# Block-sparse attention with a feed-forward layer: an ordering edge from the newest exponential on ScalarE to the score and AV groups on TensorE

## The chip, the cores and the metric

The kernel runs on one core of a Trainium2 chip, as one program. The metric is the device time of one execution in microseconds. Engines are named as in the profile: PE is TensorE (PEld its weight loads), DVE is VectorE, ACT is ScalarE, POOL is GpSimd, SP issues most DMAs. Each engine works through its own list of instructions in order; engines wait for one another by semaphores.

## The reference

```
B, H, S, D = 4, 8, 768, 64          # q, k, v; blocks of 32, 24 blocks
mask: |blk_i - blk_j| <= 1, or either block first or last, or one of 3 sampled blocks per row of blocks
scores = where(mask, q @ k.T / sqrt(D), -1e9)
attn = softmax(scores)              # exp(scores - max) / (sum + 1e-9)
x = (attn @ v) as (B*S, 512)
h = x @ w_in                        # 512 -> 2048
out = maximum(0.01 * h, h) @ w_out  # 2048 -> 512, float32
```

## The kernel before, in words

**Tiling.** Two blocks of queries (64 rows) form a tile T, 12 per batch; T = 0 holds the first and the last block, which see all 768 keys, and the 11 others see 12 gathered blocks, 384 keys. Four T of a batch make an item (256 rows), so there are 12 items. A *unit* is one T with two heads, on 128 partitions; an item has 16 units. Two units that follow one another are a *pair*: 96 pairs in all. float32 precision is kept by splitting operands into a high and a low half of 16 bits.

**A pair's way through the engines.** `scores` (line 637, matmul on line 659): per unit four matmuls of 384 keys into one PSUM bank; there are two banks (`ps_s`, two buffers), so the scores of a pair can only be written after DVE has read those of the pair before. The second unit's matmuls are emitted first. `unit_ttr` (line 666, DVE) adds the mask, scales, takes the row's extreme and leaves the result in `p`. `unit_exp` (line 677, ACT) takes the exponential of `p` with its sum. `pair_norm` (line 685, DVE), `unit_high` (line 695, ACT) and `unit_split` (line 699, DVE) make normalised probabilities `pp` in two halves; a transposing DMA (line 704, SP) turns them into `pt`, three buffers. `pair_av` (line 730, PE) multiplies by the gathered values `vg` with 24 matmuls per pair (12 per unit) into the one PSUM bank `av`, which collects the two pairs of a T. `tile_evac` (lines 737 to 748) turns a finished T into a part of the item's `x`.

**Side work.** POOL copies sampled key blocks into `kg` (line 602, two buffers), and gathers the value blocks into `vg` by indirect DMAs (line 628, two buffers; each frees when the last AV of its T is done). q, k and v of what comes next are scaled, split and transposed (`prep_q`, `prep_k`, `prep_v`); the transposes and copies of q go by DMA (lines 546 to 549). In the first part of the run the weights are decoded, scaled and split (lines 325 to 390).

**Feed-forward (FFN).** Per item eight chunks: `ffn_h` (line 765, 24 matmuls into a bank `h`), activation on ACT, DVE and POOL (lines 771 to 779) into `g`, and `ffn_o` (line 792, 12 matmuls). An item's chunks are emitted once its attention is complete and the weights they need are ready.

**What sets the order.** The outer loop (line 1041) goes over the units, one step each; a string of letters fixes what a step emits: normalise, DVE read, split, high half, exponential (`x`), scores of the next pair (`S`, in a pair's second step), activations of FFN, `ffn_o`, evacuation, AV (`a`), side work, `ffn_h`. AV of a pair comes six steps after the pair's second unit (`av_lag` and the stages before it), so the exponential that was emitted last is then that of the second unit three pairs further on. A planner then makes the lists of the engines when the program is built: it goes through its own estimate of time and issues, on each engine, the ready instruction of the best priority. Priorities follow the order of emission. The function `together` (line 164) emits a group of matmuls: the first with the priority of its place, the others with a much better one and each tied to the first by an edge that is not a semaphore, so that the planner keeps the group nearly whole. An edge of the class `NoSync` bounds only the order in which the planner issues; nothing waits for it on the chip.

Of the kernel before, what the change touches and what calls it, by code (L numbers as in the profile page):

```python
# [65 lines left out]
def tile_block_sparse_attention_ffn(  # L66
# [19 lines left out]
    nc = tc.nc  # L86
# [30 lines left out]
    def bank(name, tag="h"):  # L117
        return ps_1.tile([P, 512], F32, tag=tag, name=name, bufs={"h": 3, "av": 1}[tag])
# [42 lines left out]
        tc.cur_priority = now + 8  # L161
        return r

    def together(emits):

        now = tc.cur_priority
        begin = len(nc.cur_bb.bb.instructions)
        for n, emit in enumerate(emits):
            if n == 1:
                tc.cur_priority = now - 100000  # L170
            emit()
        new = nc.cur_bb.bb.instructions[begin:]
        for i in new[1:]:
            tc.add_manual_dep(i, new[0].name, mybir.DependencyInfo(
                mybir.DependencyClass.NoSync, mybir.DependencyReason.DATA), reason="together")
        tc.cur_priority = now + len(new)
# [378 lines left out]
    def score_scale(b, j, i, hp):  # L555

        first = j == 0 and i == 0
        hs = slice(hp, hp + 1) if first else slice(0, NP)
        nsc = sm.tile([P, NP], F32, tag="nsc", name=f"nsc_{b}_{j}_{i}_{hp}", bufs=6)
        nc.vector.tensor_scalar(  # L560
            out=nsc[:, hs], in0=kready[b, "inv"][:, hs], scalar1=qstack[b, j, i][2][:, :1], scalar2=None, op0=ALU.mult)
        for h in range(NP)[hs]:
            nscale[b, j, i, h] = nsc[:, h:h + 1]
# [73 lines left out]
    def scores(us):  # L637

        emits = []
        for u in us:  # L640
            i, c0 = u.k // 2, u.k % 2 * Q2
            require_qk(u.b, u.j, i, u.hp)
            if u.T:
                require_kg(u.b, u.T)
            key = (u.b, u.j, i, u.hp)
            if key not in nscale:
                score_scale(*key)
            u.nsc = nscale[key]
            u.sp = [ps_s.tile([P, 512], F32, tag="s", name=f"s_{u.nm}_{part}")[:, :KEYS] for part in range(u.parts)]
        for u in us[::-1]:  # L650
            i, c0 = u.k // 2, u.k % 2 * Q2
            qs, qxs, _ = qstack[u.b, u.j, i]
            for part, sp in enumerate(u.sp):
                for n, st in enumerate((qs, qxs)):
                    for hh in range(2):
                        h = 2 * u.hp + hh
                        keys = kgs[u.b, u.T][0][:, h, :] if u.T else kts[u.b][:, h, part * KEYS:(part + 1) * KEYS]
                        emits.append(lambda o=sp[hh * D:(hh + 1) * D, :], a=st[:, h, c0:c0 + Q2], k=keys, n=n:
                                     nc.tensor.matmul(o, a, k, start=(n == 0), stop=(n == 1)))  # L659
        together(emits)  # L660

    def unit_ttr(u):
        u.p = [pa.tile([P, KEYS], F32, tag="p", name=f"p_{u.nm}_{i}", bufs=CFG["p"]) for i in range(u.parts)]
# [8 lines left out]
    def unit_exp(u):  # L672

        if u.first:
            u.pair.sum = sm.tile([P, 2, 2], F32, tag="sum", name=f"sum_{u.nm}", bufs=4)
        for i in range(u.parts):
            nc.scalar.activation(  # L677
                u.p[i], u.p[i], AF.Exp, scale=-1.0, bias=u.mx[:, :1], accum_out=u.pair.sum[:, u.pi, i:i + 1])

    def pair_norm(pr):  # L680
        tot = pr.sum[:, :, 0]
        if pr.units[0].parts == 2:
            nc.vector.tensor_tensor(out=tot, in0=tot, in1=pr.sum[:, :, 1], op=ALU.add)
        pr.r = sm.tile([P, 2], F32, tag="r", name=f"r_{pr.nm}", bufs=4)
        nc.vector.tensor_scalar(out=tot, in0=tot, scalar1=1e-9, scalar2=1.0 / PSCALE, op0=ALU.add, op1=ALU.mult)  # L685
        nc.vector.reciprocal(out=pr.r, in_=tot)
# [27 lines left out]
    def pair_av(pr):  # L714

        if pr.hp == 0:
            avs[pr.item.n, pr.T] = bank(f"av_{pr.nm}", "av").rearrange("p (n l t) -> p n l t", n=NP, l=2)
        pr.av = avs[pr.item.n, pr.T]
        for u in pr.units:
            require_v(u.b, u.hp, u.T)  # L720
        emits = []
        for u in pr.units[::-1]:
            n = NCH * u.parts
            for c in range(n):
                for l in range(2):
                    for hh in range(2):
                        vt = vgs[u.b, u.T][:, c, 2 * u.hp + hh, :] if u.T else v16s[u.b, u.hp][:, c, hh, :]
                        emits.append(lambda o=pr.av[hh * D:(hh + 1) * D, u.hp], a=vt[:, l * D:(l + 1) * D],
                                     m=u.pt[c // NCH][:, :, c % NCH, hh * D:(hh + 1) * D], c=c, l=l, n=n:
                                     nc.tensor.matmul(o, a, m, start=(c == 0 and l == 0), stop=(c == n - 1 and l == 1)))  # L730
        together(emits)

    def tile_evac(pr):

# [20 lines left out]
    def ffn_h(c):  # L755
        it = c.item
        c.ph = bank(f"h_{it.nm}_{c.f}").rearrange("p (f t) -> p f t", f=2)
        emits = []
        for i in range(2):
            f = c.f + i  # L760
            b, o = f // PER, (f % PER) * P
            for d in range(NP):
                for m, (wl, xl) in enumerate(((1, 0), (1, 1), (0, 0))):
                    emits.append(lambda i=i, d=d, m=m, w=W16[:, 2 * b, d, wl, o:o + P], x=it.x[:, xl, d, :]:
                                 nc.tensor.matmul(  # L765
                                     c.ph[:, i], w, x, start=(d == 0 and m == 0), stop=(d == NP - 1 and m == 2)))
        together(emits)
# [57 lines left out]
    for b in range(B):  # L825
        for j in range(NI):
# [3 lines left out]
            for k_ in range(TPI):  # L830
                for hp in range(0, NP, 2):
                    pr = Unit()
                    pr.item, pr.k, pr.T, pr.hp, pr.nm, pr.units = it, k_, j * TPI + k_, hp, f"{it.nm}_{k_}_{hp}", []
                    for pi in range(2):
                        u = Unit()
# [18 lines left out]
    def require_qk(b, j, i, hp):  # L854
        until(("k", b, hp), lambda: (b, hp) in kready)
        until(("q", b, j, i), lambda: (b, j, i) in qstack)

    def require_kg(b, T):
        for hp in range(NP):
            until(("k", b, hp), lambda: (b, hp) in kready)  # L860
        until(("kg", b, T), lambda: (b, T) in kgs)

    def require_v(b, hp, T):
        until(("v", b), lambda: (b, hp) in v16s if T == 0 else (b, "ready") in scr)
        while T and (b, T) not in vgs:
            start_gather_v()
# [159 lines left out]
    def av_step(now=False):  # L1026
        if pend_av and (now or pend_av[0][0] <= step):
            pr = pend_av.popleft()[1]
            tlive[0] -= pr.units[0].parts
            while evs and pr.hp == 0:  # L1030
                ev_step()
            pair_av(pr)
            if pr.hp == NP - 2:
                vfree[0] += pr.T > 0
                evs.append(tile_evac(pr))
# [5 lines left out]
    for u in units:  # L1041
# [33 lines left out]
        if step == 0:  # L1075
            scores([u])
        c = aq[0] if aq else None
        for w in CFG["ord"]:
# [7 lines left out]
            elif w == "S" and step + 1 < len(units):  # L1086
                ahead = units[step + 1:step + 3]
                if not CFG["spair"]:
                    scores(ahead[:1])
                elif u.pi == 1:  # L1090
                    if any(x.parts > 1 for x in ahead):
                        for x in ahead[:1]:
                            scores([x])
                    else:
                        scores(ahead)
                elif u.parts > 1:
                    scores(ahead[:1])
            elif w == "t":
# [6 lines left out]
                unit_ttr(u)  # L1105
            elif w == "x":
                unit_exp(u)
                if u.pi == 1:
                    pend_norm.append(u.pair)
# [95 lines left out]
```

## Time and profile before

| | |
|---|---|
| three runs | 893.37 us median, 889.02 to 898.08 |
| profiled execution | 889.45 us |
| its span, first to last instruction | 887.7 us |
| mean granted PE clock | 0.948 |
| DMA | 139.25 MB, mean 157 GB/s |

Times in the profile's views count from the start of the span. A line of the timeline gives start, duration, engine, line, operation, out<-in, how many were merged (x8), and in brackets how long the engine stood idle before it and what ended that. L659 is line 659 of the kernel before. A row of waits gives who waited for whom, total us, times, longest. `s` are the scores, `mx` the extreme that the DVE read leaves, `av` the AV bank, `qs_q` and `qxs_q` the transposed queries.

### The profile page before, as it was taken

How to read it: one execution, taken by the hardware profiler on the slowest of the kernel's cores; microseconds unless marked ns; L12 is line 12 of the kernel's file. 1: busy time of each engine (PE TensorE's matmuls, PEld its weight loads, DVE VectorE, ACT ScalarE, POOL GpSimd, SP SyncE). 2: the span in 40 equal slices, each digit the busy share in tenths (PEclk: the TensorE clock that was granted, in tenths of full speed). 3: DMA queues.
4: the chain of work that ended last, by engine and by line, in shares of the span. 5: the costliest groups of instructions: out<-in, count | busy, mean ns of one | idle time of the engine just before them, and what ended most of it. 6: DMA issues, size and time to landing. Idle time of an engine off the chain costs nothing. (4 is left out here: it accounts for less than half of the span.)

```text
span 887.7 us, 19902 instructions
## 1 busy us (share of the span) xinstructions
PE 739.8 (83%) x7020; PEld 488.9 (55%) x7020; DVE 624.9 (70%) x1623; ACT 485.8 (55%) x1063; POOL 432.7 (49%) x558
## 2 busy tenths in 40 slices
PE   0234655877999998888999999999899999999997
PEld 0213433645666665555656565656556666656674
DVE  2799898997977886773857867789657677754121
ACT  3666768665655764562645846556536454543211
POOL 0046767565236465664343475476325565633221
PEclk9999555989999999999999999999999999999999
DMA  6998999967679989893558979768836596654000
GB/s 138 272 298 192 280 208 234 207 146 170 141 165 182 197 156 194 137 212 89 145 97 157 217 145 195 169 136 184 194 59 135 106 183 154 126 100 103 20 7 25
DMA packets 328450, 139.25 MB, mean 157 GB/s; under 512 B 295453, under 2 KB 307742, under 8 KB 328350
## 3 DMA queue, kind: packets, MB, share of 16 engines
q1 hardware_dynamic: 322718, 120.67, 66.8%
q0 software_dynamic: 5632, 17.31, 7.6%
q8 instruction: 55, 0.90, 0.4%
q14 instruction: 45, 0.37, 0.1%
HBM read 65.58 MB, written 12.58 MB: 88 GB/s over the span
## 5 line engine op out<-in xcount | busy, mean ns | idle before, releaser
L792 PE MATMUL o<-W,g 128*128 128x512 f16 x1152 | 276.3, 384 | 7.9 <-DVE g L778 6.0
L765 PE MATMUL h<-x,W 128*128 128x256 f16 x2304 | 275.3, 276 | 2.4 <-DVE wi_tot L140 1.1
L765 PEld LDWEIGHTS <-W 128*128 128x128 f16 x2304 | 224.9, 100 | 51.1 <-issue 12.8
L779 POOL TENSOR_TENSOR g<-ht,g 128x512 f16<-128x512 f32 x96 | 114.8, 1196 | 216.8 <-DVE g L778 169.1
L602 POOL COPY kg<-kt 128x256 f16 x264 | 131.4, 521 | 97.0 <-PE s L659 47.7
L792 PEld LDWEIGHTS <-g 128*128 128x128 f16 x1152 | 107.7, 99 | 128.9 <-issue 14.5
L677 ACT ACTIVATE p<-p,mx 128x384 f32<-128x384 f32 x208 | 125.9, 606 | 93.0 <-DVE mx L666 70.8
L699 DVE SCALAR_TENSOR_TENSOR pp<-p,r,pp 128x384 f16<-128x384 f32 x208 | 147.9, 737 | 40.4 <-ACT pp L695 39.1
L695 ACT ACTIVATE pp<-p,r 128x384 f16<-128x384 f32 x208 | 115.6, 605 | 43.8 <-issue 12.9
L628 POOL DMA_INDIRECT vg<-scr,rows x88 | 95.0, 1080 | 61.0 <-PE av L730 40.9
L774 DVE SCALAR_TENSOR_TENSOR ht<-ht 128x512 f32<-128x512 f32 x96 | 71.1, 741 | 75.3 <-ACT ht L771 74.9
L666 DVE CUSTOM_DVE_ANT_0 p<-s,em,nsc 128x384 f32<-128x384 f32 x176 | 101.9, 611 | 25.5 <-PE s L659 25.2
L730 PE MATMUL av<-pt,vg 128*64 128x128 f16 x2112 | 84.8, 230 | 20.6 <-DMA pt<-pp 15.0
L730 PEld LDWEIGHTS <-vg 128*64 128x64 f16 x2112 | 73.5, 117 | 47.3 <-issue 41.3
L771 ACT ACTIVATE ht<-h,gd 128x512 f32<-128x512 f32 x80 | 54.1, 676 | 78.8 <-PE h L765 43.4
L659 PE MATMUL s<-kg,qs_q 128*64 128x384 f16 x352 | 65.6, 368 | 25.0 <-DVE mx L666 20.2
L659 PEld LDWEIGHTS <-qs_q 128*64 128x64 f16 x416 | 28.4, 116 | 85.1 <-issue 46.1
L659 PE MATMUL s<-kg,qxs_q 128*64 128x384 f16 x352 | 64.3, 360 | 6.3 <-DMA qxs_q<-qs_q 6.3
L778 DVE CAST g<-ht 128x512 f16<-128x512 f32 x96 | 43.9, 457 | 12.4 <-PE o L792 10.3
L748 POOL TENSOR_TENSOR x<-xf,x 128x256 f16<-128x256 f32 x48 | 37.1, 773 | 27.8 <-ACT x L746 27.3
L685 DVE TENSOR_SCALAR sum<-sum 128x2 f32<-128x2 f32 x96 | 30.9, 322 | 22.0 <-ACT p L677 21.3
L534 ACT ACTIVATE qa_q<-rq 128x512 f16<-128x512 f32 x25 | 15.7, 626 | 51.8 <-DMA rq<-in_q_dram 40.3
(129 smaller groups left out, 753.6 us busy)
## 6 DMA issues: line engine op xcount, KB each, us to landing
vg<-scr SPq DMA_DIRECT2D x44, 256.0 KB, 3.9
v<-in_v_dram SPq DMA_DIRECT2D x32, 192.0 KB, 4.5
qxs_q<-qs_q SPq DMA_DIRECT2D x48, 128.0 KB, 3.1
scr<-v SPq DMA_DIRECT2D x16, 384.0 KB, 4.2
W<-in_moe_w_in_dram SPq DMA_DIRECT2D x5, 1024.0 KB, 5.9
rq<-in_q_dram SPq DMA_DIRECT2D x20, 256.0 KB, 5.3
out_dram<-ob SPq DMA_DIRECT2D x20, 256.0 KB, 3.4
rk<-in_k_dram SPq DMA_DIRECT2D x24, 192.0 KB, 4.8
```

The source lines that it names most:

```text
L602: nc.gpsimd.tensor_copy(out=kg[:, :, slot * BLOCK:(slot + 1) * BLOCK], in_=kt[:, :, bass.ds(off, BLOCK)])
L628: nc.gpsimd.indirect_dma_start(out=vg[:n_, c, :], out_offset=None, in_=scr[b][:, :], in_offset=bass.IndirectOffsetOnAxis(ap=rows[:n_, c - ...
L659: nc.tensor.matmul(o, a, k, start=(n == 0), stop=(n == 1)))
L666: nc.vector.tensor_tensor_reduce(out=u.p[i], in0=u.sp[i], in1=kgs[u.b, u.T][1] if u.T else zero.to_broadcast([P, KEYS]), scale=u.nsc, scal ...
L677: nc.scalar.activation(u.p[i], u.p[i], AF.Exp, scale=-1.0, bias=u.mx[:, :1], accum_out=u.pair.sum[:, u.pi, i:i + 1])
L695: nc.scalar.activation(pp[:, 0, :], p, AF.Copy, scale=u.r)
L699: nc.vector.scalar_tensor_tensor(out=pp[:, 1, :], in0=p, scalar=u.r, in1=pp[:, 0, :], op0=ALU.mult, op1=ALU.subtract)
L730: nc.tensor.matmul(o, a, m, start=(c == 0 and l == 0), stop=(c == n - 1 and l == 1)))
L765: nc.tensor.matmul(c.ph[:, i], w, x, start=(d == 0 and m == 0), stop=(d == NP - 1 and m == 2)))
L774: nc.vector.scalar_tensor_tensor(out=c.t, in0=c.t, scalar=0.01, in1=c.t, op0=ALU.mult, op1=ALU.max)
L779: nc.gpsimd.tensor_tensor(out=c.g[:, 1], in0=c.t, in1=c.g[:, 0], op=ALU.subtract)
L792: nc.tensor.matmul(o, a, w, start=(c.first and i == 0 and m == 0), stop=(c.last and i == 1 and m == 2)))
```

## The change

The kernel now remembers, under the key "exp", the last instruction of the newest exponential of a unit with one part (all T except T = 0), and `together` adds an edge of the class `NoSync` from the first instruction of a group to it. The groups of `scores` and of `pair_av` ask for that, those of `ffn_h` and `ffn_o` don't. "Newest" is by the order of emission: for scores it is the exponential of the unit just before, for AV that of the step in which it is emitted. After a T = 0 the name is that of an older unit.

```diff
+    newest = {}
+
+    def mark(key):
+        newest[key] = nc.cur_bb.bb.instructions[-1].name
+
+    def together(emits, after=None):
-    def together(emits):
...
         new = nc.cur_bb.bb.instructions[begin:]
+        if after in newest:
+            tc.add_manual_dep(new[0], newest[after], mybir.DependencyInfo(
+                mybir.DependencyClass.NoSync, mybir.DependencyReason.DATA), reason="order")
         for i in new[1:]:
             tc.add_manual_dep(i, new[0].name, mybir.DependencyInfo(
                 mybir.DependencyClass.NoSync, mybir.DependencyReason.DATA), reason="together")
...
     def scores(us):
...
-        together(emits)
+        together(emits, "exp")
...
     def unit_exp(u):
...
+        if u.parts == 1:
+            mark("exp")
...
     def pair_av(pr):
...
-        together(emits)
+        together(emits, "exp")
```

## The prediction

> **What bounds the kernel now.** I read the page first, then busy time by stretches, then what TensorE waited for, then the order of single instructions around the score and AV groups.
>
> ```profile
> span 887.7 us, 19902 instructions
> ...
> PE 739.8 (83%) x7020; PEld 488.9 (55%) x7020; DVE 624.9 (70%) x1623; ACT 485.8 (55%) x1063; POOL 432.7 (49%) x558
> ```
>
> ```profile
> 50.00:200.00 150.00, 87.11 (x868) 60.92 (x868) 137.98 (x319) 105.43 (x210) 100.31 (x112) 0.75 0.95 224
> 200.00:840.00 640.00, 599.24 (x5809) 392.01 (x5808) 450.77 (x1185) 347.80 (x801) 320.78 (x430) 0.99 0.74 147
> ```
>
> The columns of the second view are busy us of PE, PEld, DVE, ACT and POOL (with counts), granted clock, DMA share, GB/s. Two stages show. From 50 to 200 us PE is busy 87 of 150 us while DVE is busy 138: attention and the decoding of the weights go at DVE's pace. From 200 to 840 us PE is busy 599 of 640 us: there PE sets the time, and a microsecond in which it stands still is one added to the end, as long as FFN matmuls are there to fill it. The 41 us that are left are waits:
>
> ```profile
> PE s L659 <- DVE mx L666: 8.1, 6, 1.9
> PE s L659 <- DMA qxs_q<-qs_q: 7.8, 8, 1.7
> PE av L730 <- DMA pt<-pp: 7.5, 4, 2.9
> PE s L659 <- DMA qs_q<-qa_q: 6.9, 3, 3.2
> ```
>
> These are PE's waits from 200 us on (us in total, times, longest). PE takes its list in order, so each is a group that the plan put into the list ahead of what it needs. The first row is scores that wait until DVE has read the PSUM banks of the pair before; the third is AV that waits for the transposed probabilities.
>
> **What the change does to the order.** It adds no instruction, wait or semaphore, and removes none. Its edge goes to the first matmul of a score or AV group, and the others of the group follow that one; in the plan the group may not be issued before the newest exponential. So a group moves back on PE's list if it now stands before that exponential, and else stays. I set each group's start beside the start of its exponential. Two of these cases:
>
> ```profile
> 284.85 0.35 PE L659 MATMUL s<-kg,qs_q 128*64 128x384 f16 x2 [1.93 <-DVE mx L666]
> ```
>
> ```profile
> 287.53 0.60 ACT L677 ACTIVATE p<-p,mx 128x384 f32<-128x384 f32 x1
> ```
>
> ```profile
> 401.17 0.86 PE L730 MATMUL av<-pt,vg 128*64 128x128 f16 x24 [1.24 <-DMA pt<-pp]
> 404.39 0.86 PE L730 MATMUL av<-pt,vg 128*64 128x128 f16 x24 [2.36 <-DMA pt<-pp]
> ```
>
> ```profile
> 443.81 0.60 ACT L677 ACTIVATE p<-p,mx 128x384 f32<-128x384 f32 x1
> ```
>
> The scores at 284.85 stand 2.7 us before the exponential of their predecessor at 287.53; PE stands still 1.93 us for them. The AV at 404.39 runs 39 us before its newest exponential (443.81, of the pair three further on), and PE waits 2.36 us for its transpose. Counted over the whole timeline, 27 score groups and 29 AV groups start before their exponential; 13 and 24 of them after 200 us. Nearly all of the 8.1 and 7.5 us above falls on these groups: five score starts (7.8 us) and four AV starts (7.5 us). The edge therefore acts on the right instructions.
>
> **The sum.** Scores on DVE after 200 us: 8.1 us can go. AV on its transposes: 7.5 us. Then the clock:
>
> ```profile
> 286.20:289.60 3.40, 3.40 (x15) 2.00 (x14) 1.04 (x4) 2.81 (x8) 1.53 (x5) 0.50 1.06 206
> 385.20:388.60 3.40, 3.40 (x18) 2.42 (x17) 2.63 (x6) 2.04 (x5) 2.53 (x4) 0.51 1.06 269
> 405.60:409.00 3.40, 3.40 (x11) 1.50 (x10) 1.54 (x3) 1.12 (x3) 3.08 (x4) 0.50 0.59 165
> 535.30:538.80 3.50, 3.50 (x19) 2.11 (x19) 2.95 (x10) 3.06 (x9) 1.29 (x4) 0.51 1.01 261
> ```
>
> ```profile
> 384.19 0.86 PE L730 MATMUL av<-pt,vg 128*64 128x128 f16 x24 [2.93 <-DMA pt<-pp]
> ...
> 533.23 0.35 PE L659 MATMUL s<-kg,qs_q 128*64 128x384 f16 x2 [1.29 <-DVE mx L666]
> ```
>
> In these four stretches the granted clock is at half for 3.4 us, with PE busy throughout: 1.7 us lost each time. All come right behind waits of the two kinds (1.93 at 284.85, 2.93 at 384.19, 2.36 at 404.39, 1.29 at 533.23): 4 x 1.7 = 6.8 us more. In all 8.1 + 7.5 + 6.8 = 22.4 us.
>
> [...] The rows have the dips where the waits are, so I keep the term.
>
> How much comes back? The group that now runs first is an FFN block:
>
> ```profile
> 804.80 0.77 PE s L659 x8
> 805.58 2.69 PE o L792 x12
> ...
> 837.91 0.79 PE av L730 x24
> ...
> 841.39 7.86 PE h L765 x72
> ```
>
> These rows of the critical chain price a score group at 0.77 us, an AV group at 0.79, an o block at 2.69 and an h block at 7.86/3 = 2.6. An o block that moves forward comes to its g that much earlier, and scores that move back make DVE, ACT and the copies into kg later. No row shows this cost: its lower bound is nothing, its upper one the whole 22.4 us. I take half, for of the 22.8 us that scores wait after 200 us (8.1 + 7.8 + 6.9) two thirds end on q's DMAs, which the edge leaves alone, and such a wait often stands behind the first one. Gain: **11.2 us**.
>
> Before 200 us the first FFN matmul is at 153.8, so little can fill PE:
>
> ```profile
> L765 PE MATMUL h<-x,W x2304: 269/273/421, 153.8 to 875.0; 128*128 128x256 f16 x192
> ```
>
> ```profile
> 75.20 0.53 PE L659 MATMUL s<-kg,qs_q 128*64 128x384 f16 x2 [2.87 <-DVE mx L666]
> ...
> 150.77 0.53 PE L659 MATMUL s<-kg,qs_q 128*64 128x384 f16 x2
> ```
>
> ```profile
> 76.87 0.61 ACT L677 ACTIVATE p<-p,mx 128x384 f32<-128x384 f32 x1
> ...
> 151.65 0.60 ACT L677 ACTIVATE p<-p,mx 128x384 f32<-128x384 f32 x1
> ```
>
> Here ACT is late with weights, and 12 score groups in a row, from 75.20 (1.67 us before its exponential) to 150.77 (0.88 us), precede it, by 24 us summed. If all of that lengthened attention, with a pair each (150.77 - 75.20)/11 = 6.9 us, 3.5 pairs would slip behind 200 us, whose matmuls cost 1.56 us each: 5.5 us. On the other side PE waits in this stage:
>
> ```profile
> PE s L659 <- DVE mx L666: 20.0, 13, 5.3
> PE av L730 <- DMA pt<-pp: 8.5, 3, 5.8
> ```
>
> Scores can't run earlier through an edge; at best AV stops holding them up for 8.5 us, 1.2 pairs, 1.9 us. Between +5.5 and -1.9 I take 0: DVE is the pace, 138 of 150 us, and its work stays the same. This is the cover; without it the cost is the 5.5.
>
> Delayed AV frees vg later: The AV at 404.39, the last of its T, would come near 444; the AV of two T further on, which needs that buffer filled anew, still follows 30 us later (its second pair is at 475.43, in a row below). I cost it at nothing.
>
> The profiled execution took 889.45 us (span 887.7 and 1.75 around it): 889.45 - 11.2 = 878.2. The median of the runs, 893.37, is 3.9 higher; on its scale it is **882 us**. A measurement of this kernel (889 to 898 over three runs) tells about 1% from no change, 9 us.
>
> **Rivals.** *The plan hardly changes.* On the chip, exponentials are late partly because ACT runs behind what was planned; in the plan most groups may already stand behind them. For it: seven of the 13 late score groups lead by less than 1 us. Against it: three AVs near 401 lead by 34 to 39 us. Only their two waits (1.24 and 2.36 us) and one dip would go, 5.3 us: 888, or 893 if other waits eat it.
>
> *Attention falls behind (slower).* Each score group put behind one more block starts 2.6 us later, so its exponential and the next group too. As long as FFN of an older item is left, this costs nothing. It decides when attention's lag within an item exceeds the time between its last AV and its first h:
>
> ```profile
> 475.43 0.84 PE L730 MATMUL av<-pt,vg 128*64 128x128 f16 x24
> ...
> 486.23 1.04 PE L765 MATMUL h<-x,W 128*128 128x256 f16 x8
> ```
>
> That is 10.8 us for this item, and 841.39 - 837.91 = 3.5 for the last. If all eight groups of an item move, 8 x 2.6 - 10.8 = 10 us of empty PE; in two items 20, less the 11.2 gained: +9, 902 us. Against it: after 200 us 13 groups move over nine items, one or two each, 5 us at most.
>
> *Everything is gained.* No wait returns, and AV stops holding scores up before 200 us: 22.4 + 1.9 = 24.3, 869 us.
>
> **How the numbers follow.** Chances: the forecast (gain of 5 to 18 us) 0.39, hardly any change 0.29, behind 0.24, everything 0.08. Faster by over 1% means a gain of over 9 us: 0.33 of the forecast and all of the last, 0.41. Within 1%: 0.06 of the forecast, 0.29, and 0.03 of the slower rival, 0.38. Slower: 0.21. The range goes from 867, the full gain, to 905, the slower rival with 3 us to spare; the forecast's own is 875 to 888.
>
> **What would show it.** If right, PE's waits after 200 us for scores on DVE and AV on transposes fall from 15.6 us below 5, the score and AV groups start behind their exponentials, fewer dips of the clock are left, and waits for q and g grow by under 8 us. If scores still start ahead of the exponentials, the plan hardly changed. If PE empties ahead of an item's first h, attention fell behind. The forecast is wrong if PE's idle time after 200 us doesn't fall by 5 us at least, or if the first h comes later than 160.

## The result, and the profile after

The changed kernel takes 905.7 us (median of four runs, 903.5 to 910.8), the kernel before 895.7 over the runs made beside it. The ratio estimated from these runs is 1.0129, with a 95% interval of 1.0088 to 1.0170 (the quotient of the two medians is 1.011): slower by 1.3%, where 882 us had been forecast, with a range up to 905. The profiled execution took 905.14 us.

The page of the changed kernel, its span and the busy times:

```profile
span 903.2 us, 19915 instructions
...
PE 744.0 (82%) x7020; PEld 494.3 (55%) x7020; DVE 623.7 (69%) x1623; ACT 486.9 (54%) x1063; POOL 422.4 (47%) x558
```

The span grew by 15.5 us. PE is busy 4.2 us longer for the same 7020 matmuls, and idle 159.2 us in place of 147.9, which is 11.3 more. The 13 further instructions are semaphore instructions; the new order needs some more of them, though the edge itself is none. Busy times by stretches:

```profile
50.00:200.00 150.00, 86.07 (x863) 59.15 (x863) 139.11 (x324) 106.96 (x213) 97.09 (x111) 0.78 0.98 222
200.00:840.00 640.00, 589.09 (x5682) 389.83 (x5680) 445.91 (x1175) 345.50 (x794) 310.34 (x428) 0.97 0.73 148
```

The first 200 us are as before (86 of 150 us busy). From 200 to 840 us PE now stands still for 50.9 us (640 - 589.1); before it was 40.8, and the granted clock is 0.97 in place of 0.99. PE's waits from 200 us to the end (total, times, longest):

```profile
PE s L667 <- DMA qxs_q<-qs_q: 20.0, 6, 5.6
PE q_sum L126 <- ACT qa_q L542: 5.5, 1, 5.5
PE s L667 <- DMA qs_q<-qa_q: 5.0, 3, 2.1
PE k_sum L126 <- ACT k_k L513: 4.0, 3, 2.4
PE h L775 <- DVE q_tot L140: 3.5, 3, 1.7
PE o L802 <- ACT ob L820: 3.3, 1, 3.3
PE s L667 <- DVE mx L674: 2.5, 4, 1.0
```

The two waits that the edges aim at went down: scores on DVE's read from 8.1 to 2.5 us, and AV on its transposes from 7.5 to nothing (it has no row). In their place stand longer single waits, for q's copies (`qxs_q`, 7.8 before, 20.0 now), and for small sums in q's and k's preparation. The longest one, in the timeline of PE and of SP's queue:

```profile
443.26 0.52 PE L667 MATMUL s<-kt,qs_q 128*64 128x384 f16 x4
443.61 1.51 PE L740 MATMUL av<-pt,vg 128*64 128x128 f16 x48
450.74 0.85 PE L667 MATMUL s<-kt,qxs_q 128*64 128x384 f16 x4 [5.62 <-DMA qxs_q<-qs_q]
```

```profile
438.99 1.54 SPq L554 DMA_TRANSPOSE qs_q<-qa_q  x1
...
441.95 2.75 SPq L714 DMA_TRANSPOSE pt<-pp  x1
444.79 0.54 SPq L556 DMA_DIRECT2D qxs_q<-qs_q  x1
445.38 0.59 SPq L557 DMA_DIRECT2D qxs_q<-qs_q  x1
```

```profile
443.26 0.14 PEld L667 LDWEIGHTS <-qs_q 128*64 128x64 f16 x4 [0.57 <-DMA qs_q<-qa_q]
```

The first half of a new q block's scores starts when the transposed q lands (443.26, the third view); the second half needs the two copies of it, which SP issues only behind a transpose of `pt`, and which have landed at 450.7. The place in SP's list explains the smaller part of that: the copies were issued 1.5 us after the transposed q had landed, and landed 5.9 us after the first was issued. PE's list has nothing between the halves but 48 AV matmuls, so PE stands still for 5.6 us. In the kernel before, h, o or AV blocks stood between the halves at some q blocks (those at 345.9 and 624.2), and no wait for the copies after 200 us was over 1.7 us.

The clock follows. Three of the nine stretches between 200 us and PE's last matmul in which it is at half:

```profile
292.90:299.80 6.90, 3.40 (x54) 3.26 (x56) 5.62 (x18) 3.68 (x10) 1.16 (x1) 0.51 0.69 126
449.90:456.80 6.90, 5.58 (x22) 2.25 (x23) 5.08 (x15) 3.91 (x11) 0.89 (x1) 0.51 0.69 131
552.30:559.20 6.90, 4.07 (x31) 2.60 (x31) 2.31 (x6) 3.88 (x10) 1.79 (x2) 0.51 1.01 204
```

All nine together last 44.8 us, PE being busy for 35.5 of them; before there were five of 3.4 us, 17 us in all. Four of the nine are double stretches of 6.9 us: two at the waits of 5.5 and 5.6 us, two where two shorter waits stand close (2.1 and 1.2 us at 215 to 219, 1.65 and 3.06 at 549 to 555).

### The profile page after: what moved, and what is told of

Same layout as the page of the kernel before. It is cut to its first block, busy times and chain, and to the rows that moved or that the text cites. A ratio compares the mean times of both kernels' runs of the same rounds, so it can differ in the third digit from the quotient of the medians.

```text
span 903.2 us, 19915 instructions
## 1 busy us (share of the span) xinstructions
PE 744.0 (82%) x7020; PEld 494.3 (55%) x7020; DVE 623.7 (69%) x1623; ACT 486.9 (54%) x1063; POOL 422.4 (47%) x558
## 5 line engine op out<-in xcount | busy, mean ns | idle before, releaser
L802 PE MATMUL o<-W,g 128*128 128x512 f16 x1152 | 280.1, 388 | 9.3 <-DVE g L788 3.8
L709 DVE SCALAR_TENSOR_TENSOR pp<-p,r,pp 128x384 f16<-128x384 f32 x208 | 150.7, 754 | 44.9 <-ACT pp L705 39.3
L784 DVE SCALAR_TENSOR_TENSOR ht<-ht 128x512 f32<-128x512 f32 x96 | 68.7, 716 | 70.0 <-ACT ht L781 69.9
L781 ACT ACTIVATE ht<-h,gd 128x512 f32<-128x512 f32 x80 | 54.2, 678 | 86.3 <-PE h L775 44.8
L667 PE MATMUL s<-kg,qs_q 128*64 128x384 f16 x352 | 65.0, 371 | 26.0 <-DVE mx L674 16.2
L695 DVE TENSOR_SCALAR sum<-sum 128x2 f32<-128x2 f32 x96 | 33.5, 348 | 21.2 <-ACT p L685 20.9
```

Of the source, the lines that this page charges most:

```text
L709: nc.vector.scalar_tensor_tensor(out=pp[:, 1, :], in0=p, scalar=u.r, in1=pp[:, 0, :], op0=ALU.mult, op1=ALU.subtract)
L784: nc.vector.scalar_tensor_tensor(out=c.t, in0=c.t, scalar=0.01, in1=c.t, op0=ALU.mult, op1=ALU.max)
L802: nc.tensor.matmul(o, a, w, start=(c.first and i == 0 and m == 0), stop=(c.last and i == 1 and m == 2)))
```

## The experiments

Five theories are named in what was expected. A: the scores' edge brings waits for q's copies. B: AV's edge takes away the filling between the halves. C: whatever alters the plan gives another set of waits, and the change's cost is the accident of one plan. D: the edges cost about 1% by themselves. E: the scores' edge has a gain of its own. Each ratio is to the kernel before, with its 95% interval.

### Each edge alone, an older exponential, and q earlier

*Scores alone:* `pair_av` calls `together(emits)` again.

> The edge on the scores alone; AV as before. The changed kernel's waits of PE on scores for q's transposes and copies after 200 us are 25.0 us (before 14.7), those of AV on its transposes are gone (before 7.5). Theory A (the scores' edge puts scores right onto q's late copies): this one is slow too, ratio 1.008 to 1.02, with over 20 us of waits of scores on q after 200 us, and AV's waits on transposes are back at some 7 us. Theory B (AV's edge takes away the AV groups that stood between a q block's first scores and the matmuls that need the copies): this one is within 1% of before. Theory C (every edge reshuffles the whole plan, and which waits come is accident): anything between 0.99 and 1.02, and the change's cost isn't the sum of its halves.

Measured: 0.9956 (0.9919 to 0.9994), 893.6 us. From its PE waits after 200 us:

```profile
PE s L667 <- DMA qxs_q<-qs_q: 10.1, 5, 4.1
...
PE k_sum L126 <- ACT k_k L513: 5.0, 2, 3.4
PE s L667 <- DMA qs_q<-qa_q: 4.2, 4, 1.7
...
PE s L667 <- DVE mx L674: 3.5, 2, 3.2
```

Scores wait 14.3 us for q, as in the kernel before (14.7). Theory A falls. In this plan AV's waits for its transposes are gone as well, without an edge on AV.

*AV alone:* `scores` calls `together(emits)` again.

> The edge on AV alone; scores as before. Theory A: within 0.5% of before or faster by the 7.5 us of AV's waits (0.99 to 1.005), scores' waits on DVE still at 8 us. Theory B: slow like the change, 1.008 to 1.02, with waits on q's copies over 15 us after 200 us. Theory C: anything between 0.99 and 1.02.

Measured: 1.0039 (1.0016 to 1.0062), 900.6 us. Waits for q are 14.9 us, so B falls too; scores on DVE are at 1.9 us though no edge asks for it, and k's sums are now the first row:

```profile
PE k_sum L126 <- ACT k_k L513: 10.4, 4, 5.5
PE s L667 <- DMA qxs_q<-qs_q: 8.4, 5, 3.1
PE s L667 <- DMA qs_q<-qa_q: 6.5, 2, 4.6
```

The halves don't add up to the whole (-0.4 and +0.4% against +1.3%). Both waits that were aimed at are down in each of these plans, whichever edge it has, so that they went down is not yet the work of both edges.

*An older exponential:* both edges, to the mark before the newest.

```diff
     def mark(key):
-        newest[key] = nc.cur_bb.bb.instructions[-1].name
+        if "last" in newest:
+            newest[key] = newest["last"]
+        newest["last"] = nc.cur_bb.bb.instructions[-1].name
```

> Both edges kept, but to the exponential of a whole pair earlier than the newest. On the chip scores already stand behind that one before the change, so the edge asks nothing of them, and little of AV. Theories A and B: like before, 0.995 to 1.005. Theory C: the plan is reshuffled all the same, and the time may be up to 1.5% off on either side.

Measured: 1.0114 (1.0045 to 1.0183), 908.4 us. The expectation says a whole pair; the code goes back by one unit, and in the trace of the kernel before 16 score and 17 AV groups start ahead of that exponential, in place of 27 and 29. So it asks for about half of what the change asks, not for next to nothing. PE's order is that of the kernel before up to some 180 us; from there on it is another one, with other waits:

```profile
PE s L669 <- DVE mx L676: 12.2, 12, 2.7
PE s L669 <- DMA qs_q<-qa_q: 9.1, 4, 5.4
PE av L742 <- DVE xf L752: 5.3, 2, 3.8
```

It costs nearly as much as the change, through other waits (scores on DVE 12.2 us in place of 2.5, q's copies 2.2 in place of 20.0). C would have it so; against A and B it speaks less than had been meant.

*q earlier:* the changed kernel with `"q_at": 6` in place of 8.

> The changed kernel with the preparation of each q block started two steps earlier (q_at 8 to 6), nothing else. Theory A or B, both of which say that the price is waits for q: the waits of scores on q's copies and transposes after 200 us fall from 25.0 us to under 10, and the time falls by 10 us or more, to 1.00 or less. Theory C: other waits take their place, 1.00 to 1.02.

Measured: 1.0047 (1.0012 to 1.0082), 900.1 us. The waits for q fell from 25.0 to 3.0 us, but others came, and of the 22 us that were taken away, 5.6 us of time were won (0.8% by the ratios), about half of the 10 us that A and B asked for at least:

```profile
PE s L667 <- DVE mx L674: 14.2, 9, 3.5
PE s L667 <- DMA kt<-k_k: 5.8, 2, 4.2
PE o L802 <- DVE g L788: 3.8, 3, 1.9
...
PE s L667 <- DMA qxs_q<-qs_q: 1.9, 1, 1.9
```

### The kernel before, nudged

To see what a plan is worth by accident, the kernel before got some useless column-sized operations on DVE at one place, and no edge (`TENSOR_SCALAR` on 128x1 takes 0.13 us at line 513 and 0.15 at line 148 in the trace of the kernel before, so eight are estimated at 1.1 to 1.2 us):

```diff
                 unit_ttr(u)
+                if step == 18:
+                    for _ in range(8):
+                        nc.vector.tensor_scalar(
+                            out=u.mx[:, 1:], in0=u.mx[:, :1], scalar1=1.0, scalar2=None, op0=ALU.mult)
```

> The kernel before, without any edge, with eight column-sized DVE operations behind the DVE read of unit 18: about 1 us of DVE once, at some 110 us, and work that nobody needs. In the plan, 720 of the 821 groups on PE keep their place in the order. Theory C (a plan that is changed by anything brings other waits, and the kernel before has a good one): slower than before by 0.5 to 1.5%, or at least two of the three nudges are. Theory D (the price is the edge's own): 0.998 to 1.003, as 1 us of DVE in a stage that DVE paces is worth 0.1%.

> The same with sixteen operations behind unit 26, about 2 us of DVE at some 144 us; 711 of 821 groups keep their place. Theory C: 1.005 to 1.015, or other waits of the same sum elsewhere. Theory D: 0.998 to 1.004.

> The same with eight operations behind unit 30, about 1 us of DVE at some 157 us; 743 of 821 groups keep their place. Theory C: 1.005 to 1.015, or other waits of the same sum elsewhere. Theory D: 0.998 to 1.003.

Measured: 1.0074 (1.0037 to 1.0111), 0.9995 (0.9962 to 1.0027), 1.0153 (1.0069 to 1.0237). Two of three are slower by more than their own work, and the third of them is as slow as the change:

```profile
PE s L659 <- DVE mx L666: 16.2, 11, 5.2
PE s L659 <- DMA qxs_q<-qs_q: 12.9, 7, 3.6
PE av L730 <- DMA pt<-pp: 5.3, 4, 3.0
```

So 1.3% is within what a useless microsecond of DVE does to this kernel, and the time alone no longer asks for a cost of the edges' own. Whether they have one is left to the pairs below.

### The edges over several plans

First the scores' edge alone with two of the nudges, and both edges with a nudge:

> The scores' edge alone, with the nudge of eight column-sized DVE operations behind unit 18; 721 groups on PE keep the place that they have with the scores' edge alone. Theory E (the scores' edge has a gain of its own, which shows once the accident of the plan is averaged over nudges): 0.998 to 1.005, under the 1.0074 of the same nudge without edge, with under 5 us of waits of scores on DVE after 200 us. Theory C (only accident): no order, 0.995 to 1.015.

> The scores' edge alone, with the nudge behind unit 30; 694 groups keep their place. Theory E: 0.998 to 1.007, under the 1.0153 of the same nudge without edge. Theory C: no order, 0.995 to 1.015.

> Both edges, with the nudge behind unit 18; 789 of 827 groups keep the place of the changed kernel. Theory D (the two edges together cost 1% by themselves): 1.009 to 1.018. Theory C (the 1.3% is the accident of one plan): the mean of this one, of the other nudge and of the changed kernel is within 0.5% of the mean of the kernel before and its three nudges, 1.006, though a plan so near to the changed kernel's may share its accident.

> Both edges, with the nudge behind unit 24; 788 of 827 groups keep the place of the changed kernel. Theory D: 1.009 to 1.018. Theory C: anything between 0.998 and 1.015.

Measured: the scores' edge with nudges 1.0059 (1.0024 to 1.0095) and 1.0128 (1.0058 to 1.0199). With 0.9956 from above the three have a mean of 1.0048; the kernel before and its three nudges have 1.0056. E's figures are missed (1.0059 over 1.005, 1.0128 over 1.007, scores on DVE at 5.1 us in place of under 5). Its order is not: set beside its own partner, the scores' edge is lower each time, by 0.4, 0.15 and 0.25%, the first just clear of 1 (its interval ends at 0.9994), the two others with intervals that overlap. Three such pairs leave a small gain open and don't show one. Both edges with a nudge: 1.0127 (1.0077 to 1.0176) and 1.0159 (1.0101 to 1.0217). That is what D had put down, and C's sign failed: the mean with the changed kernel is 1.0138, 0.8% above 1.0056, where within 0.5% had been asked for. But these two have nearly the changed kernel's order (789 and 788 of 827 groups), and may share its accident, so they can't part C from D.

Then small settings that lead to plans further apart, each with and without both edges, beside `q_at` 6 without them (`k_at` 7, `v_at` 30 and `side` 1.3 in place of 6, 28 and 1.2):

> The kernel before, without the edges, with the preparation of each q block started two steps earlier. It stands beside the changed kernel with the same step, 1.0047. Theory D (edges cost some 1% by themselves): faster than that one by 0.8% or more, 0.997 or less. Theory C: no order between the two, 0.995 to 1.015.

> The kernel before with k's preparation one step later (k_at 6 to 7); 673 of 821 groups keep their place. To stand beside the same setting with both edges. Theory C: 0.998 to 1.015.

> Both edges with k_at 7; 723 of 827 groups keep the changed kernel's place. Theory D (both edges cost about 1% by themselves): over its partner without edges by 0.6% or more. Theory C (accident of the plan): the difference has either sign, under 1%.

> The kernel before with v's loads two steps later (v_at 28 to 30); 755 of 821 groups keep their place. Theory C: 0.998 to 1.015.

> Both edges with v_at 30; 709 of 827 groups keep the changed kernel's place. Theory D: over its partner without edges by 0.6% or more. Theory C: either sign, under 1%.

> The kernel before with a little more side work per step (side 1.2 to 1.3); 690 of 821 groups keep their place. Theory C: 0.99 to 1.015.

> Both edges with side 1.3; 711 of 827 groups keep the changed kernel's place. Theory D (both edges cost about 1% by themselves): over its partner without edges by 0.6% or more. Theory C (accident of the plan): either sign, under 1%.

| plan | without edges | with both | difference |
|---|---|---|---|
| as given | 1 | 1.0129 (1.0088 to 1.0170) | +1.3% |
| nudge 18 | 1.0074 (1.0037 to 1.0111) | 1.0127 (1.0077 to 1.0176) | +0.5% |
| q_at 6 | 1.0033 (1.0000 to 1.0066) | 1.0047 (1.0012 to 1.0082) | +0.1% |
| k_at 7 | 1.0027 (0.9989 to 1.0064) | 1.0061 (1.0028 to 1.0094) | +0.3% |
| v_at 30 | 1.0036 (1.0008 to 1.0065) | 1.0069 (1.0035 to 1.0102) | +0.3% |
| side 1.3 | 0.9980 (0.9938 to 1.0022) | 1.0030 (1.0002 to 1.0058) | +0.5% |

The busy rows of the pages of three pairs, without and with the edges (`k_at` 7, `v_at` 30, `side` 1.3):

```profile
PE 741.3 (83%) x7020; PEld 490.5 (55%) x7020; DVE 626.5 (70%) x1623; ACT 487.1 (54%) x1063; POOL 430.9 (48%) x558
```

```profile
PE 741.8 (83%) x7020; PEld 494.5 (55%) x7020; DVE 620.0 (69%) x1623; ACT 487.6 (54%) x1063; POOL 422.6 (47%) x558
```

```profile
PE 735.8 (83%) x7020; PEld 486.5 (55%) x7020; DVE 627.0 (70%) x1623; ACT 487.4 (55%) x1063; POOL 431.2 (48%) x558
```

```profile
PE 737.9 (82%) x7020; PEld 491.2 (55%) x7020; DVE 621.6 (69%) x1623; ACT 487.5 (54%) x1063; POOL 419.6 (47%) x558
```

```profile
PE 739.5 (83%) x7020; PEld 490.2 (55%) x7020; DVE 623.7 (70%) x1623; ACT 486.7 (55%) x1063; POOL 430.6 (48%) x558
```

```profile
PE 740.8 (83%) x7020; PEld 493.1 (55%) x7020; DVE 622.2 (69%) x1623; ACT 487.8 (54%) x1063; POOL 421.4 (47%) x558
```

The intervals overlap in every pair but the first, and at `k_at` 7 the medians even point the other way (898.7 and 898.0 us), but all six differences have one sign. The five others have a mean of 0.37%, with 0.1 to 0.5% in the single pairs; none of the last three reaches the 0.6% that D had asked for. In every pair the same matmuls take longer with the edges in the profiled execution, by 0.5 to 5.5 us. So both edges cost some 0.4% on average by themselves, as far as five pairs tell, and the rest of the 1.3%, about 0.9%, is the plan that the given settings happened to get. C holds for the greater part, D for a smaller one than it named.

The waits after 200 us, pair by pair, show what each edge does in any plan and what is accident. Those of `k_at` 7, without and with the edges:

```profile
PE s L659 <- DMA qxs_q<-qs_q: 17.0, 10, 2.7
PE s L659 <- DVE mx L666: 6.6, 6, 2.4
...
PE av L730 <- DMA pt<-pp: 3.9, 1, 3.9
```

```profile
PE s L667 <- DVE mx L674: 9.1, 5, 3.1
...
PE s L667 <- DMA qxs_q<-qs_q: 5.7, 2, 3.3
```

AV's waits on its transposes, for one, are 0.4 to 7.5 us in the six plans without the edges, and in none of the six with them is there one: AV's edge does what it was meant to. Scores' waits on DVE are 5.8 to 10.9 us without and 2.5 to 14.2 with, lower in three pairs and higher in three (with the scores' edge alone they are lower in all three of its plans, 3.5, 5.1 and 9.2 us against 8.1, 8.2 and 16.2): that they fell as far as 2.5 in the plan as given is luck of that plan. The waits for q grow in the plan as given and in its near relative, nudge 18 (14.7 to 25.0 and 15.3 to 24.8 us), and fall in the four other pairs, so those, the largest in the changed kernel, are accident too.

The scores' edge holds so loosely because it binds the planner and not the chip. In the trace of the changed kernel 21 score groups still start ahead of their exponential, 9 of them after 200 us (27 and 13 before): on the chip the two engines are not where the plan had them. One of these groups:

```profile
743.57 0.53 PE L667 MATMUL s<-kg,qs_q 128*64 128x384 f16 x2 [0.97 <-DVE mx L674]
```

```profile
745.01 0.60 ACT L685 ACTIVATE p<-p,mx 128x384 f32<-128x384 f32 x1
```

## Why the prediction was wrong, step by step

*The bound.* PE is the bound after 200 us, as said; its idle time and its longer busy time make up the difference of 15.5 us (11.3 and 4.2), and 10.1 of the 11.3 lie between 200 and 840 us.

*The targets.* Right in number, half right in mechanism: the waits that had been named fell from 15.6 to 2.5 us; "below 5" had been asked for. AV's went, and go in every plan with its edge. For the scores "the edge therefore acts on the right instructions" did not hold: 9 of their groups after 200 us still start ahead of their exponential, against the sign that had been named, and in other plans with the same edge these waits are up to 14.2 us. The prediction had the reason among its rivals (exponentials late on the chip because ACT runs behind the plan), but took it as a sign of a plan that hardly changes.

*What comes back.* This is the step that failed. "I take half" of the gain was to be lost to other waits, with all of it as the upper bound. More than all of it came back: PE's waits after 200 us rose from 40.8 to 50.9 us. They grew by 10.3 us for q alone (14.7 to 25.0), where under 8 had been asked for q and g together. The bound itself was wrong: a group taken out of a bad place changes the places behind it, and nothing holds the new waits below the old ones. Three nudges without any edge, each of a microsecond or two of work, moved the time by -0.05 to +1.5%.

*The clock.* Keeping the term was right: in the kernel before all five dips stand behind waits, of 1.29 to 3.24 us, and the changed kernel has such dips too (the last section); but it had the wrong sign. It was worked out as if each wait that goes takes its dip along and none comes, and the new waits brought 44.8 us at half clock in place of 17. What of the pairs' own 0.4% is due to the clock is not shown: no run changes the clock alone, and in the profiled executions PE's idle time grows too, by 1.9 to 5.4 us in four of the five pairs (at `k_at` 7 it falls by 1.0).

*Before 200 us.* Taken as nothing, and it was: PE is busy 86.1 us in place of 87.1, and the first h starts at 148.0, earlier than 153.8.

*vg.* Taken as nothing, and no wait for it appears among PE's.

*The rivals.* The slower one had the right side and the wrong mechanism. It asked for PE running empty between an item's last AV and its first h. For the last item these are 3.4 us apart, 3.5 before, and filled by an o block:

```profile
853.27 0.86 PE L740 MATMUL av<-pt,vg 128*64 128x128 f16 x24
854.06 2.76 PE L802 MATMUL o<-W,g 128*128 128x512 f16 x12
856.66 1.58 PE L775 MATMUL h<-x,W 128*128 128x256 f16 x13
```

"The plan hardly changes" was wrong as well: PE's order leaves that of the kernel before at some 75 us, where the first late score group had stood, and stays another one, as the waits show. The rival that was missing is that a plan made anew is a draw: against a kernel whose own plan is among the better ones (of seven other plans without edges five came out slower, by 0.3 to 1.5%, two of these with an interval that reaches 1, and two equal, 0.9980 and 0.9995), a redraw loses more often than it wins.

What stays open: why the edges cost their few tenths of a per cent. The mean granted clock over all runs is lower with them in four of the five pairs, by 0.004 to 0.009, but not at `q_at` 6 (0.942 both). That AV groups, which used to be free to fill PE's short stops, are now held behind exponentials, would give fewer and longer stops. AV's edge alone, at +0.4% and a clock of 0.938 (0.948 in the kernel before beside it), points there, where the scores' edge alone shows no cost; but that is one plan, and the scores' edge alone has a clock of 0.942 without being slower. No run moves the nine named groups alone, as the planner remakes everything behind the first of them. No version tried beats the kernel before beyond accident: the scores' edge alone has 0.9956, but 1.0059 and 1.0128 under the two nudges.

## What to carry to other kernels

Where a planner writes the engines' lists at build time, an ordering edge is first of all a new plan: the plans here lie between -0.4 and +1.6% of the kernel before, most of them above it, so measure a change against several nudged plans of both versions before its own cost or gain is believed. Look in the new trace for whether the order that was asked for is there: an edge that binds only the planner did not hold where an engine ran late (21 score groups of the changed kernel start ahead of their exponential). Waits that vanish from a list don't become time saved as long as other producers (here q's and k's preparation) are as late as before; look for what each engine meets next. A stop cost more than its length where the clock was lower behind it: in the kernel before, a wait of 1.93 us (284.85) was followed by 3.4 us at half clock in which PE was busy throughout.

## What the runs showed of the hardware

Between 200 us and PE's last matmul the granted clock fell from full to half 14 times, five times in the kernel before and nine in the changed one, each time during a wait of PE or at most 1.3 us behind the end of one. Ten of the dips lasted 3.4 us. Four, all in the changed kernel, lasted 6.9 us: at the waits of 5.50 and 5.62 us, and at two pairs of shorter ones (2.13 and 1.16 us, 1.65 and 3.06 us). Another such pair, 1.23 and 2.57 us at 790 to 794, was followed by 3.4 us at half clock. The kernel before shows the short dip behind a wait of 1.93 us, and behind 1.29 and 0.93 us close together at 533 to 535. In each of the two traces the changes of the clock lie whole multiples of 3.41 us apart (from 84.78 to 886.91 us in the kernel before, from 88.13 to 798.10 in the changed one), so the traces can be read in such steps. First the step ahead of a dip in the kernel before, then two steps in the changed kernel, of which the last is followed by no dip (behind the length of 3.41 us stands PE's busy time):

```profile
282.75:286.16 3.41, 1.32 (x16) 0.64 (x12) 3.38 (x8) 0.00 (x0) 1.77 (x3) 1.00 0.99 227
```

```profile
446.53:449.94 3.41, 0.00 (x0) 0.00 (x0) 0.00 (x0) 0.00 (x0) 0.91 (x1) 1.00 1.02 247
634.26:637.67 3.41, 1.63 (x14) 0.71 (x14) 1.28 (x4) 2.04 (x5) 2.30 (x5) 1.00 1.04 278
```

In the step ahead of each of the 14 dips PE was busy for 0.00 to 1.40 us. Of the steps at full clock that no dip followed, the least busy were the one in which the changed kernel's matmuls end (897.09), with 1.42 us, and the one at 634.26, with 1.63. That PE's busy time in a step is the cause is not shown; this is a count over two traces. A wait of 3.39 us that spans the border of two steps (635.9 to 639.3) brought no dip, one of 1.93 us within one did. In the four double dips of the changed kernel PE was busy for a share of 0.00 to 0.75 of the first step at half clock, in the ten single ones of both kernels for 0.79 and more.

The two copies that follow q's transpose at 439 us were issued 5.8 and 6.4 us after it, with a transpose of `pt` of 2.75 us in SP's queue ahead of them, and had landed 5.3 us after the second was issued: a producer that the engine's own rows don't show, and that set PE's longest wait in the changed kernel.
